# Tiles 2 and 3 projected as one 256-wide pair, and the last pieces of the output 192 and 128 columns wide

## The chip, the cores and the metric

The kernel runs on one NeuronCore of one Trainium2 chip. The metric is the device time of one execution in microseconds (us).

In this document PE is TensorE (matmuls), PEld its weight loads, DVE is VectorE, ACT is ScalarE, SP and POOL are the two other engines that issue transfers. A name such as SPq or ACTq is the queue on which an engine issues its transfers.

## The reference

`x` is 2048 rows of 640. The result is `x` plus dilated local attention (32 heads, window of 8 rows at a distance of 2) on the layer-normalised rows, plus a gated feed-forward block on the same normalised rows.

```python
def reference(A_x, A_wqkv, A_wo, B_x, B_w_gate, B_w_up, B_w_down):
    x = A_x                                  # 1 x 2048 x 640, bf16
    xn = _layernorm(x, axis=-1)
    return x + _A_ref(xn, A_wqkv, A_wo) + _B_ref(xn, B_w_gate, B_w_up, B_w_down)
    # _A_ref: q, k, v = xn @ wqkv; window softmax of q.k; weighted sum of v; @ wo
    # _B_ref: ((xn @ w_gate) * (xn @ w_up)) @ w_down
```

## The kernel before

The rows are worked in 16 tiles of 128. Each is normalised (the mean, the variance and the scaling on DVE, the square root on ACT) and transposed into `XNT`, which all matmuls read. Tiles 0 to 3 are transposed by PE and copied out of PSUM; tiles 4 to 15 are transposed by transfers that SP issues. The Q and K projections of tiles 0 to 7 come first: tiles 0 and 1 chunk by chunk as the weights arrive, tiles 2 to 5 tile by tile with matmuls 128 columns wide (`proj_part`), and tiles 6 and 7 as a pair with matmuls of 256 columns (`proj_wide`). From tile 8 on the matmuls are 512 columns wide. The last output tile ends in two pieces of 256 and 64 columns, so that little is left to add and store after the last matmul.

Helpers record every operation, and a small scheduler adds the semaphores. A lambda in the dictionary that `proj_tile` takes, such as `(3, 0): lambda: tr(2)`, puts the PE transposes of a tile before chunk 3 of that projection.

```python
    # ... cut ...

    def tp_view(t, c0, c1):
        b = tp_banks[t % 2]
        if t == 0:
            b = (6, 3, 3, 4, 4)[c0]
        if t == 1 and c0 > 1:
            b = 4
        return PS[:, b, :].bitcast(BF16)[:, c0 * 128:c1 * 128].rearrange("p (c f) -> p c f", c=c1 - c0)

    # ... cut ...

    def ln_pe(t, c0=0, c1=NCH):
        for c in range(c0, c1):
            o = tp_view(t, c, c + 1)[:, 0, :]
            i = XNS[:, t % NXN, c * 128:(c + 1) * 128]
            op("pe", (lambda o, i: lambda e: e.transpose(o, i, IDENT[:]))(o, i), r=[i, IDENT[:]], w=[o], name=f"tr{t}_{c}")

    def ln_copy(t, only=(0, 1, 2)):
        parts = ((("dve", 0, 1), ("dve", 1, 3), ("dve", 3, NCH)), (("dve", 0, 2), ("act", 2, NCH)), (("act", 0, NCH),),
                 (("act", 0, NCH),))[t]
        for k, (eng, c0, c1) in enumerate(parts):
            if k not in only:
                continue
            o = XNT[:, c0:c1, t * TS:(t + 1) * TS]
            tpv = tp_view(t, c0, c1)
            if eng == "dve":
                op("dve", (lambda o, i: lambda e: e.tensor_copy(o, i))(o, tpv), r=[tpv], w=[o], name=f"xntcp{t}_{c0}")
            else:
                op("act", (lambda o, i: lambda e: e.activation(o, i, ACT.Copy))(o, tpv), r=[tpv], w=[o],
                   name=f"xntcp{t}_{c0}")

    # ... cut ...

    def proj_part(which, t, ms, b, col):
        for c, m in [(c, m) for m in ms for c in range(NCH)]:
            o = PS[:, b, col + (m - ms[0]) * TS:col + (m - ms[0] + 1) * TS]
            l, x = wcols(which, c, m), XNT[:, c, t * TS:(t + 1) * TS]
            st, sp = c == 0, c == NCH - 1
            op("pe", (lambda o, l, x, st, sp: lambda e: e.matmul(o, l, x, start=st, stop=sp))(o, l, x, st, sp),
               r=[l, x], w=[o], name=f"pp{which}_{m}_{t}_{c}")

    # ... cut ...

    def proj_wide(which, t0, m, b, col):
        o = PS[:, b, col:col + 2 * TS]
        for c in range(NCH):
            l, x = wcols(which, c, m), XNT[:, c, t0 * TS:(t0 + 2) * TS]
            op("pe", (lambda l, x, c: lambda e: e.matmul(o, l, x, start=(c == 0), stop=(c == NCH - 1)))(l, x, c),
               r=[l, x], w=[o], name=f"pw{which}_{m}_{t0}_{c}")

    # ... cut ...

    bm = 1
    proj_tile(0, [(0, 0)], bm, {(4, 0): lambda: ln_pe(1, 0, 2), (4, 3): lambda: tr(1, 2)})
    part_evac(0, 0, 1, 0, 4, 0, 0)
    proj_tile(0, [(1, 2)], bm)
    part_evac(0, 1, 1, 0, 4, 2, 0)
    ln_apply(3)
    proj_tile(1, [(0, 3), (1, 4)], bm, {(3, 0): lambda: tr(2), (4, 0): lambda: tr(3)})
    ln_start(4)
    for t in (0, 1):
        part_evac(1, t, 1, 0, 4, 3 + t, 0)
    ln_pace(12.0)
    for u in (0, 1):
        part_evac(u, 0, 2, 4, 1, bm, 2 * u * TS)
    tp = 11.9
    bank_ring[:] = [5, 0, 6, 7, 2, 1, 3, 4]
    for t0 in (2, 4):
        bm = bank()
        for which, dt in ((0, 0), (1, 0), (0, 1), (1, 1)):
            t = t0 + dt
            b = bank()
            proj_part(which, t, (0, 1), b, 0)
            proj_part(which, t, (2, 3), b, 2 * TS)
            proj_part(which, t, (4,), bm, (2 * which + dt) * TS)
            part_evac(which, t, 1, 0, 4, b, 0)
            tp += 1.4
            if (which, dt) == (1, 1):
                for u in (0, 1):
                    part_evac(u, t0, 2, 4, 1, bm, 2 * u * TS)
            ln_pace(tp)
    bank_ring[:] = [6, 7, 2, 3, 4, 5, 0, 1]
    for g in range(5):
        b = bank()
        if g == 2:
            proj_wide(0, 6, 4, b, 0)
            proj_wide(1, 6, 4, b, 2 * TS)
            part_evac(0, 6, 2, 4, 1, b, 0)
            part_evac(1, 6, 2, 4, 1, b, 2 * TS)
        else:
            which, m = ((0, 0), (0, 2), None, (1, 0), (1, 2))[g]
            proj_wide(which, 6, m, b, 0)
            proj_wide(which, 6, m + 1, b, 2 * TS)
            part_evac(which, 6, 2, m, 2, b, 0)
        tp += 1.11
        ln_pace(tp)
    ln_pace(1e9)
    bank()
    k_seam()

    # ... cut ...

    def tail(t, nb):
        j, rows = t // 4, slice((t % 4) * TS, (t % 4 + 1) * TS)
        flush_h(0)
        n = NF + NCH
        last = t == NT - 1
        parts = ((0, DHALF - 64), (DHALF - 64, 64)) if last and nb == 1 else ((0, DHALF),)
        for h, wid in parts:
            b = bank()
            c0 = nb * DHALF + h
            # ... 17 matmuls into PS[:, b, 0:wid]: 12 from WD, 5 from WO ...
            o = FOUT[:, t % NFO, cols]
            xr = XR[:, t % NXR, cols]
            op("dve", (lambda o, xr, b, wid: lambda e: e.tensor_tensor(o, PS[:, b, 0:wid], xr, ALU.add))(o, xr, b, wid),
               r=[PS[:, b, :], xr], w=[o], name=f"fin{t}_{nb}")
            if last:
                eng = "act" if c0 == DHALF else "sp"
                stores.append(dma(ohbm[t * TS:(t + 1) * TS, cols], o, r=[o], name=f"odma{t}_{c0}", eng=eng))
```

## Time and profile before

| what | value | read from |
|---|---|---|
| time | 254.32 us (254.29 to 254.47, 3 runs) | the runs |
| PE busy | 248.1 of 252.4 us, clock 1.0 | busy times |
| PE on the chain | 6.94 to 250.17 us, no real gap | chain of waits |
| 128-wide projections, tiles 2 to 5 | 11.17 us for 200, 55.85 ns each | chain of waits |
| 256-wide projections, tiles 6 and 7 | 5.46 us for 50, 109.2 ns each | chain of waits |
| last add, 64 columns | 224 ns | groups |

The busy times on the profile's page of the kernel before, engine by engine with the share of the span:

```profile
PE 248.1 (98%) x1607; PEld 149.2 (59%) x1622; DVE 215.1 (85%) x254; ACT 113.9 (45%) x202; POOL 35.9 (14%) x44
```

The chain of waits of the kernel before, in order of time. It is followed back from the last instruction; each line is the start, the length, and what the time went to (L487 is `proj_part`, L507 `proj_wide`, L472 the 512-wide projections, L677 the output matmuls, L691 the last add):

```profile
12.83 11.17 PE PS L487 x200
24.00 5.46 PE PS L507 x50
29.46 0.05 issue
29.51 10.74 PE PS L472 x49
...
194.70 55.48 PE PS L677 x425
250.17 0.02 issue
250.20 0.22 DVE FOUT L691
```

PE runs from one group into the next. The "issue" pieces of 0.05 us come with groups of 49 matmuls where the program has 50: a record is missing there, and PE did not stand still. With PE this full, work that is taken off another engine is worth nothing, unless PE would wait for it.

The groups of instructions of the kernel before that the change touches, with shapes kept apart. After the bar stand the busy time and the mean ns of one instruction; the mean of a matmul is the length of its own pass through the array, and because the passes overlap, the cost of one is read from the chain and not from here:

```profile
L487 PE MATMUL PS<-XNT,WQKV 128*128 128x128 bf16 x200 | 11.3, 219 | 0.0
...
L507 PE MATMUL PS<-XNT,WQKV 128*128 128x256 bf16 x50 | 5.6, 272 | 0.0
...
L691 DVE TENSOR_TENSOR FOUT<-PS,XR 128x256 bf16<-128x256 f32 x1 | 0.4, 424 | 1.4 <-PE PS L677 1.4
...
L691 DVE TENSOR_TENSOR FOUT<-PS,XR 128x64 bf16<-128x64 f32 x1 | 0.2, 224 | 0.1
```

### The profile page before, as it was taken

How to read it: one execution, taken by the hardware profiler on the slowest of the kernel's cores; microseconds unless marked ns; L12 is line 12 of the kernel's file. 1: busy time of each engine (PE TensorE's matmuls, PEld its weight loads, DVE VectorE, ACT ScalarE, POOL GpSimd, SP SyncE). 2: the span in 40 equal slices, each digit the busy share in tenths (PEclk: the TensorE clock that was granted, in tenths of full speed). 3: DMA queues.
4: the chain of work that ended last, by engine and by line, in shares of the span. 5: the costliest groups of instructions: out<-in, count | busy, mean ns of one | idle time of the engine just before them, and what ended most of it. 6: DMA issues, size and time to landing. Idle time of an engine off the chain costs nothing.

```text
span 252.4 us, 3908 instructions
## 1 busy us (share of the span) xinstructions
PE 248.1 (98%) x1607; PEld 149.2 (59%) x1622; DVE 215.1 (85%) x254; ACT 113.9 (45%) x202; POOL 35.9 (14%) x44
## 2 busy tenths in 40 slices
PE   8999999999999999999999999999999999999996
PEld 3999855555544444444444457764444777777775
DVE  4899799999999954999999974899999999995221
ACT  5486675555555557555555552225555112112000
POOL 1000001044425331003411100101000010111000
DMA  6988789956777562536379931393000021330511
GB/s 201 297 177 164 117 205 395 277 109 114 134 137 128 92 125 44 199 134 124 57 138 314 429 101 23 37 347 55 0 0 0 3 32 20 55 45 9 104 52 52
DMA packets 25664, 31.83 MB, mean 126 GB/s; under 512 B 9744, under 2 KB 22160, under 8 KB 25616
## 3 DMA queue, kind: packets, MB, share of 16 engines
q1 hardware_dynamic: 19120, 22.15, 28.9%
q0 software_dynamic: 6240, 9.31, 23.0%
q8 instruction: 12, 0.20, 0.3%
q10 hardware_dynamic: 288, 0.15, 0.2%
q14 instruction: 4, 0.03, 0.0%
HBM read 14.42 MB, written 4.59 MB: 75 GB/s over the span
## 4 chain that ended last, share of the span: by engine, by line
PE 96%; ACT 1%; DMA 1%; DVE 1%; issue 0%
PE PS L646 41%; PE PS L677 29%; PE PS L472 17%; PE PS L487 4%; PE PS L507 2%; PE PS L500 2%; DMA XST<-in_A_x_dram 1%; ACT XNS L391 0%; PE PS L431 0%; ACT XNS L389 0%; DVE STATS L369 0%; DVE STATS L375 0%; DVE XNS L416 0%; ACT SD L394 0%; ACT SD L382 0%
## 5 line engine op out<-in xcount | busy, mean ns | idle before, releaser
L646 PE MATMUL PS<-XNT,WU 128*128 128x512 bf16 x240 | 59.6, 379 | 0.0
L646 PE MATMUL PS<-XNT,WG 128*128 128x512 bf16 x229 | 57.3, 379 | 0.6
L613 DVE TENSOR_TENSOR PVB<-VO,ATB 128x10240 f16<-128x10240 bf16 x8 | 43.9, 5492 | 0.1
L677 PE MATMUL PS<-WD,HT 128*128 128x320 bf16 (+2 forms) x300 | 43.2, 294 | 0.0
L472 PE MATMUL PS<-XNT,WQKV 128*128 128x512 bf16 x196 | 43.0, 379 | 0.2
L646 PEld LDWEIGHTS PS<-XNT,WU 128*128 128x128 bf16 x240 | 23.5, 98 | 28.3
L646 PEld LDWEIGHTS PS<-XNT,WG 128*128 128x128 bf16 x240 | 23.5, 98 | 28.1
L648 ACT ACTIVATE USX<-PS 128x512 bf16<-128x512 f32 x48 | 28.7, 597 | 22.2 <-PE PS L646 21.7
L677 PEld LDWEIGHTS PS<-WD,HT 128*128 128x128 bf16 x300 | 28.7, 98 | 11.0
L472 PEld LDWEIGHTS PS<-XNT,WQKV 128*128 128x128 bf16 x200 | 23.5, 118 | 19.5
L608 DVE TENSOR_TENSOR PVB<-PVB 128x5120 f16<-128x5120 f16 (+1 forms) x16 | 34.6, 2160 | 0.3
L541 POOL DMA_DIRECT2D LOG<-PE x24 | 21.9, 939 | 60.9 <-DMA LOG<-PE 60.9
L648 ACT ACTIVATE HT<-PS 128x512 bf16<-128x512 f32 x36 | 21.5, 597 | 16.8 <-PE PS L646 16.8
L686 ACT ACTIVATE FACC<-PS 128x640 f16<-128x640 f32 x12 | 8.4, 703 | 44.1 <-PE PS L677 44.1
L677 PE MATMUL PS<-WO,VO 128*128 128x320 bf16 (+2 forms) x165 | 27.1, 295 | 0.0
L677 PEld LDWEIGHTS PS<-WO,VO 128*128 128x128 bf16 x165 | 15.9, 98 | 5.9
L530 DVE TENSOR_TENSOR PP<-QH,KH 128x2048 f16<-128x2048 bf16 x16 | 19.1, 1221 | 0.0
L530 DVE TENSOR_TENSOR TMP<-QH,KH 128x2048 f16<-128x2048 bf16 x16 | 19.0, 1221 | 0.0
L535 DVE TENSOR_TENSOR PP<-PP,TMP 128x4096 f16<-128x4096 f16 x8 | 18.3, 2292 | 0.2
L701 POOL DMA_DIRECT2D out_dram<-FACC x6 | 7.1, 1186 | 74.7 <-ACT FACC L686 74.7
L541 POOL DMA_DIRECT2D PE<-PP x8 | 8.7, 1089 | 61.3 <-DVE PP L536 61.3
L691 DVE TENSOR_TENSOR FOUT<-PS,XR 128x320 bf16<-128x320 f32 (+2 forms) x9 | 4.1, 454 | 15.3 <-PE PS L677 15.2
(67 smaller groups left out, 229.7 us busy)
## 6 DMA issues: line engine op xcount, KB each, us to landing
PE<-PP POOLq DMA_DIRECT2D x8, 512.0 KB, 5.0
ATB<-LOG SPq DMA_DIRECT2D x8, 512.0 KB, 4.3
LOG<-PE POOLq DMA_DIRECT2D x24, 128.0 KB, 2.7
WG<-in_B_w_gate_dram SPq DMA_DIRECT2D x1, 1920.0 KB, 9.3
WU<-in_B_w_up_dram SPq DMA_DIRECT2D x1, 1920.0 KB, 17.3
WD<-in_B_w_down_dram SPq DMA_DIRECT2D x1, 1920.0 KB, 10.1
out_dram<-in_A_x_dram SPq DMA_DIRECT2D x1, 1920.0 KB, 11.0
out_dram<-FACC POOLq DMA_DIRECT2D x6, 320.0 KB, 4.6
```

The costliest lines, as they stand in the source:

```text
L472: op("pe", (lambda l, x, c: lambda e: e.matmul(PS[:, b, :], l, x, start=(c == 0), stop=(c == NCH - 1)))(l, x, c), r=[l, x], w=[PS[:, b, :] ...
L487: op("pe", (lambda o, l, x, st, sp: lambda e: e.matmul(o, l, x, start=st, stop=sp))(o, l, x, st, sp), r=[l, x], w=[o], name=f"pp{which}_{m ...
L530: return (1.22, lambda: op("dve", lambda e: e.tensor_tensor(o, qw, kw, ALU.mult), r=[q, k], w=[o], name=f"prod{h}_{p}_{c}"))
L535: (2.3, lambda: op("dve", lambda e: e.tensor_tensor(a, a, b, ALU.add), r=[a, b], w=[a], name=f"psum{h}_{p}")),
L541: op("pool", lambda e: e.dma_start(o, i, accum_op=ALU.add), r=[o, i], w=[o], dma=True, name=name)
L608: return lambda: op("dve", lambda e: e.tensor_tensor(o, x, y, ALU.add), r=[x, y], w=[o], name=f"{name}_{b}")
L613: lambda: op("dve", lambda e: e.tensor_tensor(PVB[:], vw, aw, ALU.mult), r=[v, a], w=[PVB[:]], name=f"pv_{b}")),
L646: op("pe", (lambda l, x, c: lambda e: e.matmul(PS[:, b, :], l, x, start=(c == 0), stop=(c == NCH - 1)))(l, x, c), r=[l, x], w=[PS[:, b, :] ...
L648: op("act", lambda e: e.activation(o, PS[:, b, :], ACT.Copy), r=[PS[:, b, :]], w=[o], name=f"guev{which}_{m}_{j}")
L677: op("pe", (lambda l, x, i, b, wid: lambda e: e.matmul(PS[:, b, 0:wid], l, x, start=(i == 0), stop=(i == n - 1)))(l, x, i, b, wid), r=[l, ...
L686: op("act", (lambda o, i: lambda e: e.activation(o, i, ACT.Copy))(o, i), r=[PS[:, b - 1, :], PS[:, b, :]], w=[o], name=f"fin{t}")
L701: stores.append(op("pool", lambda e: e.dma_start(d, f, accum_op=ALU.add), r=[f, ("out",)], w=[("out", t)], dma=True, name=f"oacc{t}"))
```

## The change

The intent: project tiles 2 and 3 as one pair with half as many matmuls of twice the width. The pair needs both tiles' transposes before its first matmul, so these move one chunk of ten matmuls earlier, and the copy of tile 2 out of PSUM is shared by DVE and ACT, so that ACT is free sooner for tile 3. With the pair come another order of the copies out of PSUM (`part_evac`), another order of PSUM banks, and other points at which later tiles are normalised (`ln_pace`). Separately, the last two pieces become 192 and 128 columns.

```diff
--- before.py
+++ after.py
@@ -360,6 +360,8 @@
             b = (6, 3, 3, 4, 4)[c0]
         if t == 1 and c0 > 1:
             b = 4
+        if t == 2 and c0 > 2:
+            b = 5
         return PS[:, b, :].bitcast(BF16)[:, c0 * 128:c1 * 128].rearrange("p (c f) -> p c f", c=c1 - c0)
 
     def ln_stats_a(t):
@@ -431,8 +433,8 @@
             op("pe", (lambda o, i: lambda e: e.transpose(o, i, IDENT[:]))(o, i), r=[i, IDENT[:]], w=[o], name=f"tr{t}_{c}")
 
     def ln_copy(t, only=(0, 1, 2)):
-        parts = ((("dve", 0, 1), ("dve", 1, 3), ("dve", 3, NCH)), (("dve", 0, 2), ("act", 2, NCH)), (("act", 0, NCH),),
-                 (("act", 0, NCH),))[t]
+        parts = ((("dve", 0, 1), ("dve", 1, 3), ("dve", 3, NCH)), (("dve", 0, 2), ("act", 2, NCH)),
+                 (("dve", 0, 3), ("act", 3, NCH)), (("act", 0, NCH),))[t]
         for k, (eng, c0, c1) in enumerate(parts):
             if k not in only:
                 continue
@@ -664,7 +666,7 @@
         flush_h(0)
         n = NF + NCH
         last = t == NT - 1
-        parts = ((0, DHALF - 64), (DHALF - 64, 64)) if last and nb == 1 else ((0, DHALF),)
+        parts = ((0, DHALF - 128), (DHALF - 128, 128)) if last and nb == 1 else ((0, DHALF),)
         for h, wid in parts:
             b = bank()
             c0 = nb * DHALF + h
@@ -760,7 +762,7 @@
     proj_tile(0, [(1, 2)], bm)
     part_evac(0, 1, 1, 0, 4, 2, 0)
     ln_apply(3)
-    proj_tile(1, [(0, 3), (1, 4)], bm, {(3, 0): lambda: tr(2), (4, 0): lambda: tr(3)})
+    proj_tile(1, [(0, 3), (1, 4)], bm, {(2, 0): lambda: tr(2), (3, 0): lambda: tr(3)})
     ln_start(4)
     for t in (0, 1):
         part_evac(1, t, 1, 0, 4, 3 + t, 0)
@@ -768,36 +770,40 @@
     for u in (0, 1):
         part_evac(u, 0, 2, 4, 1, bm, 2 * u * TS)
     tp = 11.9
-    bank_ring[:] = [5, 0, 6, 7, 2, 1, 3, 4]
-    for t0 in (2, 4):
-        bm = bank()
-        for which, dt in ((0, 0), (1, 0), (0, 1), (1, 1)):
-            t = t0 + dt
+
+    def wide_pair(t0):
+        nonlocal tp
+        for g in range(5):
             b = bank()
-            proj_part(which, t, (0, 1), b, 0)
-            proj_part(which, t, (2, 3), b, 2 * TS)
-            proj_part(which, t, (4,), bm, (2 * which + dt) * TS)
-            part_evac(which, t, 1, 0, 4, b, 0)
-            tp += 1.4
-            if (which, dt) == (1, 1):
-                for u in (0, 1):
-                    part_evac(u, t0, 2, 4, 1, bm, 2 * u * TS)
+            if g == 2:
+                proj_wide(0, t0, 4, b, 0)
+                proj_wide(1, t0, 4, b, 2 * TS)
+                part_evac(0, t0, 2, 4, 1, b, 0)
+                part_evac(1, t0, 2, 4, 1, b, 2 * TS)
+            else:
+                which, m = ((0, 0), (0, 2), None, (1, 0), (1, 2))[g]
+                proj_wide(which, t0, m, b, 0)
+                proj_wide(which, t0, m + 1, b, 2 * TS)
+                part_evac(which, t0, 2, m, 2, b, 0)
+            tp += 1.11
             ln_pace(tp)
+
+    bank_ring[:] = [5, 0, 2, 6, 7, 1, 3, 4]
+    wide_pair(2)
+    bm = bank()
+    for which, t in ((0, 4), (1, 4), (0, 5), (1, 5)):
+        b = bank()
+        proj_part(which, t, (0, 1), b, 0)
+        proj_part(which, t, (2, 3), b, 2 * TS)
+        proj_part(which, t, (4,), bm, (2 * which + t - 4) * TS)
+        part_evac(which, t, 1, 0, 4, b, 0)
+        tp += 1.4
+        if (which, t) == (1, 5):
+            for u in (0, 1):
+                part_evac(u, 4, 2, 4, 1, bm, 2 * u * TS)
+        ln_pace(tp)
     bank_ring[:] = [6, 7, 2, 3, 4, 5, 0, 1]
-    for g in range(5):
-        b = bank()
-        if g == 2:
-            proj_wide(0, 6, 4, b, 0)
-            proj_wide(1, 6, 4, b, 2 * TS)
-            part_evac(0, 6, 2, 4, 1, b, 0)
-            part_evac(1, 6, 2, 4, 1, b, 2 * TS)
-        else:
-            which, m = ((0, 0), (0, 2), None, (1, 0), (1, 2))[g]
-            proj_wide(which, 6, m, b, 0)
-            proj_wide(which, 6, m + 1, b, 2 * TS)
-            part_evac(which, 6, 2, m, 2, b, 0)
-        tp += 1.11
-        ln_pace(tp)
+    wide_pair(6)
     ln_pace(1e9)
     bank()
     k_seam()
```

## The prediction

> **What bounds the kernel.** TensorE. The busy times show PE busy 248.1 of 252.4 us (98%), granted clock 1.0. The chain of waits runs through PE without a real gap from 6.94 to 250.17 us. So only PE's own work, a new PE wait, or what follows 250.17 us can move the time.
>
> **PE work removed.** Tiles 2 and 3 took 100 matmuls of width 128; now 50 of width 256. In the chain, 200 matmuls of 128 took 11.17 us (55.85 ns each) and 50 of 256 took 5.46 us (109.2 ns each). The same columns cost 5.585 us before, 5.46 us after: 0.125 us saved, all on the chain. The Trainium skill, "TensorE: Matmul & The Clock Gate" (Part 1, "Wait — 56ns, not 53.3ns?"), puts a warm matmul at N/2.4 GHz plus about 2.5 ns; both figures agree, and 50 x 2.5 ns is the whole saving. Weight loads halve too, but run beside the matmuls.
>
> **Last pieces.** Widths 256+64 become 192+128. By the timeline the 256-wide matmuls cost 109.2 ns, the 64-wide about 29 ns: 17 x 138.4 ns = 2.35 us. An estimate by the same rule for 192 and 128 is 82.5 + 55.8 = 138.3 ns: no change on PE. VectorE then adds the last piece: 224 ns at 64 columns, 424 ns at 256, so about 290 ns at 128 (interpolated): +0.067 us on the chain. That piece's store grows from 16 to 32 KB; landings were 1.5 us (16 KB), 1.6 us (64 and 80 KB), so at most +0.05 us. The first piece's store leaves about 0.5 us sooner, which may remove overlap between the two stores. Tail in sum: +0.05 to +0.1 us, half or more of the gain.
>
> **New waits.** The wide pair needs both tiles' copies before its first matmul (12.67 us on the timeline); before, only tile 2 was needed. Hence the transposes move up a chunk (0.56 us) and tile 2's copy is split. Worked through: tile 3 is normalised by 10.87 us, its transposes end near 11.71; ScalarE is free by then (its part of tile 2, about 0.39 us, ends near 11.55), and tile 3's copy (0.70 us) ends near 12.45: 0.2 us of slack. VectorE's part of tile 2 (about 0.35 us) falls into 0.47 us in which it waited for a load. DMA-transposed tiles 7 and 11 landed about 1 us before PE wanted them; PE arrives only 0.13 us sooner. VectorE's last attention sums ended 11 us before PE read them.
>
> **Prediction.** 254.32 - 0.125 + 0.07 = about 254.25 us; 8 times in 10 between 253.95 and 254.6. Faster by over 2%: 0.5%; within 2%: 99%; slower by over 2%: 0.5%.
>
> **What would show each step.** The separate tiles' 128-wide group falls from 200 to 100 matmuls, the 256-wide grows from 50 to 100 at 109 ns each on the chain; no PE wait near 12.7 us; PE's last matmul ends 0.12 us sooner (250.04 us); the 192- and 128-wide groups take 2.35 us together; the last add takes 0.29 us; the last store lands in 1.5 to 1.6 us; the span shrinks by 0.0 to 0.15 us.
>
> **What would make it wrong.** Tile 3's copy ends late, so PE waits at 12.7 us; a DMA transpose of tiles 4 to 11 shifts by over 1 us; the last store's landing depends on bytes per row or the store beside it more than its size suggests, moving the end by tenths; the spread (0.18 us in three runs) is larger than the net effect, so its sign may not show.

## The result, and the profile after

| | before | after |
|---|---|---|
| median, runs of the prediction's comparison | 254.34 us (6 runs) | 254.25 us (6 runs, one of them slow; 254.11 us over the five fast ones) |
| ratio of fast runs | | 0.9989, interval 0.9973 to 1.0005 |
| second comparison, 5 rounds | 254.34 us (11 runs) | 253.99 us (6 runs), ratio 0.9977 |
| third comparison, 5 rounds | 254.37 us (12 runs) | 254.03 us (6 runs), ratio 0.9983 |

A ratio is the mean time of one kernel's fast runs over that of the other's, so it is not quite the ratio of the medians quoted. The third comparison is not independent of the second: eleven of its twelve "before" runs are those of the second. Three of these eleven took 255.03 to 256.34 us, which pulls the ratios down; the medians of the second comparison differ by 0.14%, not 0.23%.

The first profile of the changed kernel fell into the slow run (376.75 us at a clock of 0.66), so it is not used for durations. All that follows is read from a profile of a fast run of the same kernel, taken in the first experiment. Its busy times:

```profile
PE 247.8 (98%) x1557; PEld 149.1 (59%) x1572; DVE 215.2 (85%) x255; ACT 114.1 (45%) x202; POOL 35.8 (14%) x44
```

Its chain of waits (line numbers are two or so higher: L509 is `proj_wide`, L489 `proj_part`, L474 the 512-wide projections, L679 the output matmuls, L693 the last add):

```profile
11.62 1.12 PE PS L502 x20
12.73 5.46 PE PS L509 x50
18.19 5.58 PE PS L489 x100
23.77 5.46 PE PS L509 x50
29.23 0.05 issue
29.29 10.74 PE PS L474 x49
...
194.47 55.48 PE PS L679 x425
249.95 0.02 issue
249.97 0.29 DVE FOUT L693
```

The three pairs took 11.17 + 5.46 = 16.63 us before and 5.46 + 5.58 + 5.46 = 16.50 us after: 0.13 us less. The output matmuls take 55.48 us in both, so the new widths of the last pieces cost PE nothing. The pair starts the moment the projection of tile 1 ends (11.62 + 1.12 against 12.73), so there is no new wait. The groups of the same profile:

```profile
L509 PE MATMUL PS<-XNT,WQKV 128*128 128x256 bf16 x100 | 11.2, 272 | 0.0
...
L489 PE MATMUL PS<-XNT,WQKV 128*128 128x128 bf16 x100 | 5.7, 219 | 0.0
...
L693 DVE TENSOR_TENSOR FOUT<-PS,XR 128x192 bf16<-128x192 f32 x1 | 0.4, 358 | 0.9 <-PE PS L679 0.9
...
L693 DVE TENSOR_TENSOR FOUT<-PS,XR 128x128 bf16<-128x128 f32 x1 | 0.3, 291 | 0.6 <-PE PS L679 0.6
```

The last add took 0.067 us longer, as forecast. But the end of PE (249.95 after, 250.17 before) moved by 0.22 us and the span (252.19 after, 252.42 before) by 0.23 us, so the longer add was paid back somewhere, and 0.1 us of the shift was there before tile 2 began. The experiments ask where.

### The profile page after: what moved, and what is told of

The parts are those of the page before. It is cut to its first block, busy times and chain, and to the rows that moved or that the text cites. A ratio compares the mean times of both kernels' runs of the same rounds, so it can differ in the third digit from the quotient of the medians.

```text
span 375.0 us, 3825 instructions
## 1 busy us (share of the span) xinstructions
PE 371.7 (99%) x1572; PEld 184.2 (49%) x1572; DVE 219.0 (58%) x255; ACT 114.5 (31%) x202; POOL 35.8 (10%) x44
## 4 chain that ended last, share of the span: by engine, by line
PE 99%; DVE 0%; issue 0%
PE PS L648 42%; PE PS L679 30%; PE PS L474 17%; PE PS L509 4%; PE PS L502 2%; PE PS L489 2%; PE PS L452 1%; PE PS L433 0%; DVE FOUT L693 0%; DVE ZERO L296 0%; DVE EPSC L297 0%
## 5 line engine op out<-in xcount | busy, mean ns | idle before, releaser
L648 PE MATMUL PS<-XNT,WU 128*128 128x512 bf16 x240 | 87.3, 513 | 0.0
L648 PE MATMUL PS<-XNT,WG 128*128 128x512 bf16 x240 | 87.3, 513 | 0.0
L474 PE MATMUL PS<-XNT,WQKV 128*128 128x512 bf16 x200 | 65.4, 513 | 0.0
L679 PE MATMUL PS<-WD,HT 128*128 128x320 bf16 (+2 forms) x300 | 63.4, 382 | 0.0
L648 PEld LDWEIGHTS PS<-XNT,WG 128*128 128x128 bf16 x240 | 29.3, 122 | 48.8 <-issue 48.7
L648 PEld LDWEIGHTS PS<-XNT,WU 128*128 128x128 bf16 x240 | 29.0, 121 | 49.3 <-issue 49.3
L679 PEld LDWEIGHTS PS<-WD,HT 128*128 128x128 bf16 x300 | 35.5, 120 | 24.1 <-issue 0.9
L653 DVE TENSOR_TENSOR HT<-HT,USX 128x512 bf16<-128x512 bf16 x36 | 15.2, 422 | 54.8 <-ACT USX L650 54.8
L474 PEld LDWEIGHTS PS<-XNT,WQKV 128*128 128x128 bf16 x200 | 26.9, 135 | 38.0 <-issue 37.7
L679 PE MATMUL PS<-WO,VO 128*128 128x320 bf16 (+2 forms) x165 | 38.8, 384 | 0.0
L693 DVE TENSOR_TENSOR FOUT<-PS,XR 128x320 bf16<-128x320 f32 (+2 forms) x9 | 4.1, 454 | 51.7 <-PE PS L679 51.7
L679 PEld LDWEIGHTS PS<-WO,VO 128*128 128x128 bf16 x165 | 19.7, 121 | 13.0
```

What stands on the lines that cost most here:

```text
L474: op("pe", (lambda l, x, c: lambda e: e.matmul(PS[:, b, :], l, x, start=(c == 0), stop=(c == NCH - 1)))(l, x, c), r=[l, x], w=[PS[:, b, :] ...
L648: op("pe", (lambda l, x, c: lambda e: e.matmul(PS[:, b, :], l, x, start=(c == 0), stop=(c == NCH - 1)))(l, x, c), r=[l, x], w=[PS[:, b, :] ...
L653: h_pending.append(lambda: op("dve", lambda e: e.tensor_tensor(h, h, o, ALU.mult), r=[h, o], w=[h], name=f"h{m}_{j}"))
L679: op("pe", (lambda l, x, i, b, wid: lambda e: e.matmul(PS[:, b, 0:wid], l, x, start=(i == 0), stop=(i == n - 1)))(l, x, i, b, wid), r=[l, ...
```

## The experiments

Theory T says that the 2.5 ns per matmul saved on PE is the gain, less what the tail costs. Its rivals are R1, that the gain comes from the stores at the end, and R2, that there is no gain and the difference is scatter. Each run was profiled; those with rounds were timed against the kernel before on the same chip. All runs gave correct results.

### 1 and 2: the changed kernel and the kernel before, again

No edit in either.

> The changed kernel again, because its recorded profile fell into an execution with a granted clock of 0.66. Theory T (PE width): PE's last matmul ends 0.12 us sooner than before (250.04 to 250.06 us on the trace, if the first 6.94 us take as long), the last add takes 0.29 us in place of 0.22, no PE wait near 12.7 us; time about 0.06 us under before. Rival R1 (tail): PE's end does not move, and the gain comes from the last stores landing sooner. Rival R2 (no gain at all): the two differences cancel to within 0.02 us and the measured ratio of 0.9989 is scatter of the first microseconds.

> The kernel before against itself: the floor of the comparison. All theories: ratio 1.000, interval within 0.0015 of it. The second profile shows which stretch scatters between executions of one program. I expect the stretch up to the first projections at about 6.9 us (loads from memory) to scatter by 0.1 us or more, the PE stretch by under 0.02 us, the tail by under 0.1 us.

Measured: the changed kernel 253.99 us, ratio 0.9977 (0.9951 to 1.0002). The kernel before against itself 254.37 us, ratio 0.9991 (0.9964 to 1.0018), with runs from 253.92 to 256.34 us among both sets. The interval of a kernel against itself thus reaches 0.27% to each side, 0.7 us, which is more than the whole effect: times alone cannot settle this, and the profiles have to be compared stretch by stretch.

The profile of the kernel before fell into a run of 255.13 us, with a span 0.92 us longer than in its first profile. Its list of waits of PE (who waited for whom; total, times and longest in us):

```profile
PE PS L450 <- DVE EPSC L297: 1.0, 1, 1.0
PE PS L500 <- DVE XNS L416: 0.5, 1, 0.5
PE PS L472 <- DMA XNT<-XNS: 0.3, 1, 0.3
PE PS L500 <- DMA WQKV<-in_A_wqkv_dram: 0.3, 1, 0.3
```

The chain of the same profile, where PE turns to the 512-wide projections:

```profile
22.66 7.47 DMA XNT<-XNS x2
30.13 0.29 issue
30.43 10.74 PE PS L472 x49
```

Of the 0.92 us, 0.65 us lie before the projections of tile 2 (they began at 13.48 us on the chain and not at 12.83), and they come with waits for the first loads of `x` and of the weights. The other 0.27 us is a wait for the transposes that SP issues: tile 11 landed at 30.13 us and PE had been ready. In the first profile of before it landed at 28.46 us, 1.05 us ahead of PE. My expectation had the start scatter, but it gave the PE stretch no scatter at all; that was wrong for this kernel, because of this wait.

### 3 and 4: each half of the change alone

Run 3 has the whole change except the line of the last pieces; run 4 has only that line.

```diff
 # run 3, on the changed kernel
-        parts = ((0, DHALF - 128), (DHALF - 128, 128)) if last and nb == 1 else ((0, DHALF),)
+        parts = ((0, DHALF - 64), (DHALF - 64, 64)) if last and nb == 1 else ((0, DHALF),)
 # run 4, on the kernel before: the same line the other way round
```

> The wide pair and its copies alone, with the last pieces left at 256 and 64. T: PE's last matmul ends 0.12 us sooner, the tail is that of before (last add 0.22 us), so 0.12 us under before and 0.06 us under the full change. R1: no gain. R2: no gain.

> The last pieces of 192 and 128 alone, on the kernel before. T: PE's end unchanged within 0.01 us, last add 0.29 us in place of 0.22, last store landing within 0.05 us of before's: 0.07 us slower than before. R1: faster than before by about the whole gain, 0.1 to 0.3 us, because the last two stores overlap less. R2: same.

Measured: the pair alone 254.13 us, ratio 0.9979 (0.9952 to 1.0007); the pieces alone 254.38 us, ratio 0.9991 (0.9965 to 1.0016), which is what the kernel before gave against itself. By the medians the gain goes with the pair and not with the pieces, against R1, but these differences lie within the noise. In stretches it is clearer: the three pairs took 16.50 us with the pair and 16.63 us with the pieces alone. Nor is it given back later: from the start of tile 2's projections to the end of PE, the first profile of before took 237.33 us and run 4 237.32, while runs 1, 3, 9 and 12, all with the wide pair, took 237.20 or 237.21. The profile with the pair alone happened to wait 1.1 us for the weights at its start, so its span of 253.0 us says nothing about the change.

The last chain lines of the run with the pieces alone:

```profile
250.38 0.02 issue
250.40 0.29 DVE FOUT L691
```

The tail, from the end of PE to the end of the span, was expected to grow by 0.07 us with the pieces. It did not:

| run | last pieces | end of PE | end of last add | last store landed | add to landing | end of PE to end of span |
|---|---|---|---|---|---|---|
| before | 256, 64 | 250.16 | 250.42 | 251.97 | 1.55 | 2.26 |
| 3, pair alone | 256, 64 | 250.73 | 250.99 | 252.54 | 1.55 | 2.27 |
| 1, whole change | 192, 128 | 249.94 | 250.26 | 251.74 | 1.48 | 2.26 |
| 4, pieces alone | 192, 128 | 250.36 | 250.69 | 252.16 | 1.47 | 2.25 |

(All in us from the span's start; the end of PE and the landings are single records of the trace, of which the page shows only rounded sums.) The add is 0.067 us longer and the store, though twice as large, lands 0.07 to 0.08 us sooner after it. The forecast growth of the tail did not come at all; run 7 takes it apart.

### 5, 6 and 9: which of the protections is needed

Run 5 takes both protections away, run 9 only the split copy. Run 6 puts both into the kernel before, with its narrow pair.

```diff
 # run 5, on the changed kernel (run 9: the first two hunks only)
-        if t == 2 and c0 > 2:
-            b = 5
-                 (("dve", 0, 3), ("act", 3, NCH)), (("act", 0, NCH),))[t]
+                 (("act", 0, NCH),), (("act", 0, NCH),))[t]
-    ... {(2, 0): lambda: tr(2), (3, 0): lambda: tr(3)})
+    ... {(3, 0): lambda: tr(2), (4, 0): lambda: tr(3)})
 # run 6, on the kernel before: these hunks the other way round
```

> The full change without its two protections: the transposes of tiles 2 and 3 back at their old places, and tile 2 copied by ScalarE alone. If the copy of tile 3 is what the wide pair depends on (theory T), PE waits for it: transposes of tile 3 end about 12.2 us, ScalarE copies 0.70 us from there, so the first wide matmul starts about 13.0 us in place of 12.6 and PE's end is 0.3 to 0.4 us later than with the full change, 0.2 to 0.3 us later than before. Rival: the protections do nothing, PE shows no wait and the time is that of the full change.

> Only the earlier transposes and the split copy of tile 2, on the kernel before with its narrow pair and its last pieces. T: nothing on PE's chain changes, PE's stretch from the second projection tile to its end is that of before within 0.02 us, time as before. Second question, the slack at 29.5 us: the DMA transpose of tile 11 landed 1.05 us before PE wanted it in one profile of before, PE waited 0.33 us for it in another, and the slack was 1.55 us in both fast profiles with the wide pair. If the order of ScalarE's square roots in the wide pair gives the slack (theory S), it stays under 1.1 us here; if the earlier copies give it (rival), it is about 1.5 us here.

> The full change with the earlier transposes but tile 2 copied by ScalarE alone, as before. ScalarE is free at about 11.0 us, tile 2's copy takes 0.70 us and tile 3's another 0.70 us less a small overlap, so tile 3's copy ends at about 12.4 us as with the split. Theory U (only the earlier transposes matter): no PE wait near 12.7 us, PE's three pairs take 16.50 us, time as the full change. Rival (the split matters): PE waits 0.1 to 0.3 us there as in the run without both protections.

Measured: without both, 254.46 us, ratio 1.0005 (0.9989 to 1.0020); with the copies alone on the kernel before, 254.37 us, ratio 1.0007 (0.9988 to 1.0027); with early transposes but one copy, 254.15 us, ratio 0.9981 (0.9945 to 1.0017). PE's waits in run 5:

```profile
PE PS L450 <- DVE EPSC L297: 1.0, 1, 1.0
PE PS L507 <- ACT XNT L444: 0.2, 1, 0.2
```

ACT in run 5 and then in run 9, from the timeline, each line with its start and length. L444 is the two copies of tiles 2 and 3, merged:

```profile
11.74 1.30 ACT L444 ACTIVATE XNT<-PS 128x640 bf16<-128x640 bf16 x2
```

```profile
11.21 1.41 ACT L444 ACTIVATE XNT<-PS 128x640 bf16<-128x640 bf16 x2
```

In run 5 the copies end at 13.04 us and the pair begins at 13.09, after 0.24 us of idle PE by the timeline. The pair's chain piece reads 5.65 us there and not 5.46, mostly because after a wait the chain counts from the start of the first matmul, and otherwise from the end of the matmul before, 0.16 us later (12.57 and 12.73 us in run 1). By PE's end, 250.49 us, the run is 0.3 us behind the first profile of before, though it began the transposes of tile 2 only 0.02 us later (11.01 against 10.99 us). So the wide pair without help loses more than it saves. In run 9 the copies end at 12.62 us; the pair's first matmul starts at 12.83 us on the timeline, with no wait, and the three pairs take 16.50 us. The earlier transposes are the protection; the split copy is not needed. Theory U holds.

Run 6 answers the question of the slack before the 512-wide projections, which is the start of those on the chain less the landing of tile 11's transpose:

| kernel | pair of tiles 2 and 3 | tile 8 normalised, after tile 4 | long issues of SP before tile 11's | slack of tile 11 |
|---|---|---|---|---|
| before, first profile | narrow | 6.30 | 1 | 1.05 |
| before, run 2 | narrow | 5.68 | 2 | none, PE waited 0.3 |
| run 4, pieces alone | narrow | 6.30 | 2 | 0.53 |
| run 6, copies alone | narrow | 6.20 | 2 | 0.20 |
| run 7, gap (below) | narrow | 6.30 | 1 | 1.08 |
| run 1, whole change | wide | 5.42 | 1 | 1.55 |
| run 3, pair alone | wide | 5.72 | 1 | 1.55 |
| run 5, no protections | wide | 5.46 | 1 | 1.48 |
| run 9, early, one copy | wide | 5.65 | 1 | 2.10 |
| run 12, whole change | wide | 5.41 | 1 | 1.18 |

(All in us but the count; an issue is called long here when it took over 1.6 us. Starts are modelled by the profiler. The weight load of the first 512-wide matmul begins 0.27 us before the start that the chain gives, at 29.15 against 29.42 us in run 7, so a slack under about 0.27 us is already a short wait.) With the wide pair (and tiles 4 and 5 narrow) the slack was 1.1 to 2.1 us; with the narrow pair it was 1.08 us at the most and once negative. The ranges nearly touch (run 10, below, had 1.12 us with the wide pair). The copies alone gave 0.20 us and not the 1.5 us that the rival asked for, so the rival falls. In run 6 the weight load even waited for tile 11, which landed at 29.20 us: PE took 237.37 us from the start of tile 2's projections to its end, 0.04 us more than before, and not within 0.02 us of it as expected. In run 2 everything was late, tile 4 too, so its third column is short.

Theory S, that the order of ScalarE's square roots gives the slack, is not shown by this. The square root that tile 8 needs did begin sooner in run 1 (17.65 us) than in before (19.19 us), where it stood behind copies of the projections. But the transpose of tile 8 did not wait for it. SP issues the transposes and loads one after the other, and it came to that of tile 8 1.38 us after tile 8 was normalised in before and 1.04 us after in run 1; in all ten profiles it was about 1.0 us or more, and for tiles 9 to 11 it was at least 0.9 us. What differed most is how long SP took for single issues. (SP also waited for tile 6 to be normalised, 0.35 us in before and 0.06 in run 1, but 0.37 us with the wide pair of run 3.) Most of the transposes took it 1.2 to 1.3 us, but single issues took 1.7 to 2.3 us: in before that of tile 6, in run 1 that of tile 8, in run 12 a load. The issues of tiles 4 to 7 show it, first in before, then in run 1 (start and length):

```profile
13.90 6.51 SPq L420 DMA_TRANSPOSE XNT<-XNS  x4
```

```profile
13.90 5.28 SPq L422 DMA_TRANSPOSE XNT<-XNS  x4
```

Three of the five narrow profiles had two such long issues before tile 11's, tiles 6 and 10 each time, and they are the three with the least slack; each wide profile had one. The narrow profiles with one (1.05 and 1.08 us) come close to the least of the wide ones (1.18 us here, 1.12 in run 10). Why an issue takes longer, and whether the wide pair makes this rarer, stays open.

### 7: a gap between the last two stores

Six idle matmuls stand between the last two pieces of the kernel before.

```diff
+            if h > 0:
+                z = ZERO[:, 0:1].to_broadcast([128, JB])      # zeros, 512 wide
+                for _ in range(6):
+                    op("pe", ... e.matmul(PS[:, (b + 4) % 8, :], ZERO[:], z, start=True, stop=True) ...)
```

> The kernel before with six idle 512-wide matmuls (about 1.3 us, estimate from 216 ns each) between its last two pieces, so that the store of the 256 columns lands before that of the last 64 is issued. The store of 64 columns landed 1.55 us after its add in before (beside the other store), that of 128 columns 1.48 us after its add in the full change (the other store had nearly landed). If the overlap with the other store cost the 0.07 us (theory O), the 64 columns land 1.45 to 1.49 us after their add here; if rows of 128 bytes are slower than rows of 256 (rival W), 1.53 us or more.

Measured: one look (state unknown, granted clock 1.0), 255.51 us; the gap took 1.30 us. The last add ended at 251.69 us and the store of 64 columns landed at 253.14 us: 1.45 us, where before had 1.55. In the three other profiles with these last pieces (runs 2, 3 and 6) it was 1.55 or 1.56, so the one profile with the gap stands well apart. Theory O holds and W falls, for a row of 128 bytes is not slower than one of 256. This splits the term of the tail: the overlap had cost 0.10 us, and the larger store by itself costs about 0.03 us (1.48 us in the whole change, where the stores do not overlap, against 1.45). With the 0.067 us of the add these sum to nothing, as measured. The transfers of the two kernels, issue to landing, first before and then with the gap:

```profile
out_dram<-FOUT SPq DMA_DIRECT2D x1, 16.0 KB, 1.5
```

```profile
out_dram<-FOUT SPq DMA_DIRECT2D x1, 16.0 KB, 1.4
```

What overlaps is not the data. The trace's transfer records show that the data of the 64 columns were through 1.09 us after the add in before and 1.08 us with the gap. Each store is complete when 16 completion signals have come, which arrive 12 to 14 ns apart. In before the other store's signals came from 251.58 to 251.78 us, and those of the last store from 251.79 to 251.97 us: they stood in line. With the gap, and in the whole change (other store 250.77 to 250.97, last 251.56 to 251.74), they did not. One thing was not as I had meant it: with the gap, a single late signal of the other store came at 252.42 us, after the last store had been issued, but well before that store's first signal at 252.96 us.

### 8 and 11: all three pairs wide

Run 8 replaces the narrow pair of tiles 4 and 5 too. Run 11 also moves three loads of `x` behind later transposes.

```diff
 # run 8, on the changed kernel
-    bm = bank()
-    for which, t in ((0, 4), (1, 4), (0, 5), (1, 5)):
-        ...
+    wide_pair(4)
 # run 11, in addition
-        if t == 7:
+        if t == 10:
             x_load(13)
             x_load2(14)
```

> The full change with tiles 4 and 5 as a wide pair too, so that all three pairs are 256 wide. T: another 50 x 2.5 ns = 0.125 us off PE's work. But this pair needs tile 5's DMA transpose at once, which landed 18.12 us in the fast profile of the change, where PE comes to the pair at 18.19: no slack. If the landing is as there, PE's end is 0.12 us sooner; if it is as in the profiles of before (19.85 us), PE waits up to 1.6 us. I expect a wait of 0 to 0.5 us and a time within 0.3 us of the full change.

> All three pairs wide, and the loads of the last three x tiles issued after the DMA transpose of tile 10 in place of that of tile 7, so that the transposes of tiles 8 to 10 leave sooner. All wide alone had only 0.14 us between the landing of tile 11 and PE's need. T: three pairs in 16.40 us as there, tile 11 lands 0.5 us or more before PE's need, time 0.1 us under the full change, 0.25 us under before. It would be wrong if the late loads hold up the normalising of tile 13.

Measured: all wide 254.19 us, ratio 0.9994 (0.9981 to 1.0008); with the loads moved 254.21 us, ratio 0.9985 (0.9959 to 1.0010). The three pairs of run 8 on its chain:

```profile
12.70 16.40 PE PS L509 x150
29.10 43.26 PE PS L474 x200
```

That is 16.40 us against 16.50, so theory T's further 0.1 us is there, and tile 5 landed at 17.95 us in time. But tile 11 landed at 28.96 us, only 0.14 us before the start that the chain gives, when the first weight load of the 512-wide projections was already due, and the list of waits of run 8 has this line:

```profile
PEld PS L474 <- DMA XNT<-XNS: 0.2, 1, 0.2
```

The 512-wide projections took 43.26 us, where run 5 took 43.17. From the start of the pairs to the end of PE run 8 took 237.20 us, as the changed kernel did: this wait took back what the third pair had saved, and no gain shows in the times. In run 11 the three pairs took 16.51 us, and one weight load waited for a transpose, so that PE took 237.21 us in all, again no less:

```profile
PEld PS L509 <- DMA XNT<-XNS: 0.2, 1, 0.2
```

The moved loads also held up the normalising of tiles 12 and 13 as I had feared: DVE waited 3.5 us for a load in one piece, and the attention products began at 31.98 us where run 12 began them at 29.59. Neither kernel is shown to beat the changed one.

### 10 and 12: the width effect amplified, and the change once more

Run 10 cuts each 512-wide projection matmul into two of 256; run 12 is the changed kernel without an edit, on the same chip.

```diff
-            op("pe", ... e.matmul(PS[:, b, :], l, x, start=(c == 0), stop=(c == NCH - 1)) ...)
+            for s in (0, 256):
+                op("pe", ... e.matmul(PS[:, b, s:s + 256], l, x[:, s:s + 256],
+                                      start=(c + s == 0), stop=(c == NCH - 1 and s > 0)) ...)
```

> Amplification of the width effect, the other way round: on the full change, each of the 200 projection matmuls of 512 columns cut into two of 256 with the same weights. T: a fixed cost of about 2.6 ns per matmul (two of 109.2 ns against one of 215.8 ns by the chain), so that stretch grows from 43.2 us to 43.7 us and the time by 0.5 us, to 254.5 to 254.7. Rival (the cost goes with the columns only, and the 0.13 us came from elsewhere): no growth.

> The full change once more, on the same chip as the three above. T: three pairs in 16.50 us, span less the end of PE 2.26 us; slack of tile 11 about 1.5 us; time 0.1 to 0.35 us under before.

Measured: run 10 took 254.81 us and run 12 254.03 us, ratios 1.0010 (0.9974 to 1.0047) and 0.9983 (0.9956 to 1.0009). The chain of run 10 over the halved stretch:

```profile
29.12 43.66 PE PS L475 x400
```

Run 1 crossed the same stretch in 72.45 - 29.29 = 43.16 us, so 200 more matmuls cost 0.50 us, 2.5 ns each. T holds four times larger, and the rival falls. (Each added matmul brought its own weight load, 1772 of them against 1572 in run 12, as each matmul that the change removed took one with it; so the 2.5 ns are those of a matmul with its load, and no run here separates the two.) Run 12 had 16.50 us for the three pairs and 2.26 us from the end of PE to the end of the span, as run 1.

## Why the prediction was right or wrong

- **What bounds the kernel: right.** In before and in the changed kernel PE ran without a gap after the first loads, except for the wait in run 2.
- **PE work removed, 0.125 us: right.** The three pairs went from 16.62 or 16.63 to 16.50 us in every profile where PE did not wait before or within them, and the fixed cost of 2.5 ns per matmul showed again over 200 matmuls (0.50 us). The Trainium skill, "TensorE: Matmul & The Clock Gate", Part 1, gives N/2.4 GHz plus about 2.5 ns, and 55.85 and 109.2 ns agree.
- **Last pieces, nothing on PE: right.** 55.48 us of output matmuls in both.
- **Last add, +0.067 us: right.** 224 ns became 291 ns.
- **The store: wrong, and this is the mis-sized term.** The prediction put "at most +0.05 us" on the last store and "+0.05 to +0.1 us" on the tail. The store measured 0.07 us less and the tail 0.00 to -0.01 us. The part for the size was right, about +0.03 us. What failed is that the prediction named the overlap of the two stores as something that might be removed and counted nothing for it: the gap run shows that it had cost 0.10 us, and the records that the completion signals stand in line. So the net of the two halves is -0.13 us or a little more, not -0.06 us.
- **New waits: right in the result.** The slack of tile 3's copy was put at 0.2 us; the copy ended at 12.35 us (11.65 + 0.70) and PE began at 12.57 us by the timeline. Run 5 shows that the wait would have come without the earlier transposes. Of the two protections, the split copy did nothing for PE.
- **The transposes of the later tiles: incomplete.** The prediction read from one profile that tile 11 lands 1 us early. Over five profiles with the narrow pair the slack ran from 1.08 us to a wait of 0.3 us, and six profiles with the wide pair and the narrow pair of tiles 4 and 5 had at least 1.1 us (run 10 had 1.12). The prediction did not see this scatter. The least slack came with two long issues of SP; that the wide pair makes these rarer is not shown.
- **The time: right in the number, in part by luck.** It said 254.25 us, between 253.95 and 254.6. The comparison's median of 254.25 contains the slow run; over its fast runs the median is 254.11, and later comparisons gave 253.99 and 254.03. The range also holds the time of the kernel before, so the hit says little about the mechanism: the stretches do.

What stays open: on one chip the medians of runs 1 and 12 together (12 runs, 254.02 us) lie 0.35 us under those of the kernel before (18 runs, 254.37 us), and the stretches that repeat account for 0.13 to 0.14 us. The rarer wait for tile 11 would add to it, but only one profile of before caught it, and the start of tile 2's projections scattered from 12.6 to 13.5 us among the profiles. Whether the other 0.2 us is real was not settled.

## What to carry to other kernels

On a kernel that its matmuls fill, fewer and wider matmuls are worth their fixed cost each, here 2.5 ns, if nothing new is waited for; look up how early the newly needed tile is ready, and move its producers first, as without that the wait was larger than the gain. Follow a saving to the end of the chain: in run 8 the next wait took it all back. When an effect is a twentieth of a per cent, compare stretches of the trace between fixed points, because the start and the waits for transfers scatter by more than the effect. Measure the slack of a transfer in several profiles, for one profile shows only one draw; and near the end of a kernel let the stores finish one after the other, so that the last one's completion does not stand behind another's.

## What the Trainium skill lacked or had wrong

- "TensorE: Matmul & The Clock Gate", "Back-to-back issue gap", gives a sustained spacing of about 81 ns at 128 columns and about 131 ns at 512 for streams with a weight load before every matmul, and says the simple formula misses there. In this kernel, with a weight load before each, 200 matmuls of 128 took 55.85 ns each, 256 columns 109.2 ns, and 512 columns 215.8 ns (43.16 us for 200): the simple formula held and those two figures did not.
- "DMA: Bandwidth & Descriptors", "Anatomy of one DMA", written for transfers that GpSimd issues, speaks of about 100 ns for the semaphore update and of a semaphore write that is essentially free, and "Why a DMA increments its semaphore by 16 and not by 1" says each engine adds one. That such an increment lands only after every earlier write of its DMA engine, across its queues, stands in "Queues, rings and completion order", and the order seen here agrees. What this costs when two stores meet no page says: here the signals came 12 to 14 ns apart, and the last store completed 0.10 us later when another store's signals were just ahead (1.55 against 1.45 us).
- "VectorE: DVE Perf Modes", the table of the errata section, gives 120 cycles plus the columns at 0.96 GHz for a PSUM source, which is 192 ns at 64 columns and 258 ns at 128. The adds here took 224 and 291 ns, 32 to 33 ns more at both widths; the slope agrees. The formula that the section gives below the table for an fp32 `tensor_tensor` add, (N+151)/0.96, fits: it gives 224, 291, 357 and 424 ns at 64, 128, 192 and 256 columns, where the adds took 224, 291, 358 and 424. The section does not say that it holds for a PSUM source too.
